# A new order for the opening of a fused attention and gated-MLP kernel, with eight PSUM banks instead of six up to the first output tile

## The chip, the cores, the metric

One core of a Trainium2 chip. The metric is the device time of one execution in microseconds (us); less is better. Times inside a trace are counted from the first instruction of the program, and the span of a trace is about 1.8 us shorter than the time of the run that it profiles.

Names used below: PE is TensorE, DVE is VectorE, ACT is ScalarE, POOL is GpSimd. A *bank* is one of the eight 128x512 float32 tiles of PSUM into which PE writes its results. A *slice* is one pass of four 128x512 matmuls that makes gate and value of 128 hidden features for one batch (`gv`). A *projection unit* (`c` or `u`) multiplies the small state with a block of columns of both weights (`c`) or of one (`u`). The *steady part* begins with slice 4 of batch 2 and runs to the end.

## The reference

```python
# x (8, 8, 512, 64), state (8, 8, 32, 64)
scores = scale * x @ state^T ;  a = softmax(scores) ;  xread = a @ state
scores2 = scale * state @ x^T ; a2 = softmax(scores2) ; sread = a2 @ x
y = concat([xread, sread], axis=2) -> rows of (B*S, H*D) = (4352, 512)
out = (relu(y @ w_gate) * (y @ w_val)) @ w_out        # d_ff = 1536, float32 result
```

The softmax works over 32 state entries, so `xread @ w` is computed as `a @ (state @ w)`: the projection units make `U = state @ w`, and a slice multiplies the transposed softmax with a block of `U`.

## The kernel before

The opening is written by hand as a list of words. Each word is a step; the digits after `@` are the PSUM banks that it takes, and a bank comes free when the step that evicts it has run.

```python
def bank(name, kind="r"):
    if given:
        n = given.pop(0)                       # the digits after "@"
    elif kind == "spare":
        n = 6 + turn["o"] % 2
    else:
        n = turn["r"] % 6 if kind == "r" else 6 + turn["o"] % 2   # steady part: a ring of six, two for outputs
        turn[kind] += 1
    return psum.tile([128, 512], FP32, name=name, tag=f"b{n}")

def x_load(b, part, parts):                    # dx: x in bf16, from the software queue of POOL
    ...
    nc.gpsimd.dma_start(out=xb[b][:, :, hs]..., in_=x[b, hs]...)

def x_T2(b, half):                             # xT2: PE transposes of x
    ...
    nc.tensor.transpose(ps[64 * h2:64 * h2 + 64, c, j], xb[b][:, c, 4 * half + 2 * j + h2], id128)

def state_conv(g, half, eng):                  # stc: state to bf16, on POOL for the later groups
    dst, src, keep = st_b[:, g % 3, :, half], st_f[:, g], odd[:, half:half + 1]
    ...
def state_T(g): ...                            # stT: PE transposes of a state group
def spin(n, cols=512):                         # warming matmuls with no use of their result
    for i in range(n):
        nc.tensor.matmul(warm_ps[:, 0:cols], warm[:, 0:128], warm[:, 0:cols], start=True, stop=True)

program = """
dx.1.0.2 dx.1.1.2 stc.0.0.act stc.0.1.dve spin.7 stT.0@0 xc.0.0.dve dw.0.0.128 sto.0.act ...
... c.1.512.256@54 mu.0.2 gv.1.2@21 ... c.0.512.256@30 re.1.2 gv.1.5@45 ...
... c.0.1024.256@41 c.0.1280.256@35 ... xT2.2.0@2 stc.1.0.pool ... xT2.2.1@0 stc.1.1.pool ...
... gv.0.5@41 ... gv.0.10@53 ... stT.1@2 ...
"""
```

Other words: `dw` loads a block of weight columns, `ds` the rest of the state, `do` the output weight; `sc` scores, `ex` exponential, `nr` sums and reciprocals, `nx` scaling; `aT`/`ao` transposes of the softmax; `co`/`uo` evictions of projection units; `re`/`mu` ReLU on ACT and product on DVE after a slice; `o` a third of an output tile; `sr`/`sn` the state read.

The softmax here doesn't subtract the row's maximum and nothing guards it: scores larger than these inputs give would overflow.

Of the kernel before, what the change touches and what calls it, by code (L numbers as in the profile page):

```python
# [16 lines left out]
def kernel(  # L17
# [52 lines left out]
    stT = const.tile([128, B, NJ, 64], BF16, name="stT")  # L70
# [5 lines left out]
    xf, xb, xT, e_sn, a_sn, ANS, U, hsb, sr_sb = {}, {}, {}, {}, {}, {}, {}, {}, {}  # L76
# [362 lines left out]
             "c": c_unit, "co": c_out, "u": u_unit, "uo": u_out, "gv": gv, "re": relu, "mu": mult, "o": out_part,  # L439
             "of": fin_x, "xn": x_next, "xp": x_pad, "sr": sr_mm, "sn": sr_norm}  # L440
    program = """
    dx.1.0.2 dx.1.1.2 stc.0.0.act stc.0.1.dve spin.7 stT.0@0 xc.0.0.dve dw.0.0.128 sto.0.act dw.1.0.128 on xc.0.1.dve
    spin.3 xT.0.1@1 dw.0.128.128 xT.0.0@2 xo.0.1.dve xo.0.0.act dw.1.128.128 spin.3 sc.0.0@3 dw.0.256.256 ex.0.0
    spin.1 xT.0.2@4 xT.0.3@5 xo.0.2.dve dw.1.256.256 xo.0.3.act nr.0.0 spin.3 sc.0.1@0 dw.0.512.256 xT2.1.0@1 ex.0.1
    nx.0.0 xo2.1.0.act nr.0.1 dw.1.512.256 spin.2 xT2.1.1@2 xo2.1.1.act sc.1.0@3 dw.0.768.256 nx.0.1 ex.1.0
    dw.1.768.256 spin.2 c.1.0.128@45 c.0.0.128@01 co.1.0.128.0.dve aT.0.1@2 co.0.0.128.0.act aT.0.0@3 co.1.0.128.1.dve
    co.0.0.128.1.act dw.0.1024.256 sc.1.1@4 ao.0.1.dve ao.0.0.act nr.1.0 ex.1.1 dw.1.1024.256 spin.2 c.0.128.128@05
    gv.0.0@12 co.0.128.128.1.act nr.1.1 co.0.128.128.0.act nx.1.0.pool re.0.0 gv.0.1@34 mu.0.0 re.0.1 nx.1.1.pool
    c.1.128.128@50 mu.0.1 co.1.128.128.1.act c.0.256.256@12 co.1.128.128.0.act c.1.256.256@30 dw.0.1280.256
    co.0.256.256.0.dve co.0.256.256.1.act aT.1.1@5 aT.1.0@4 co.1.256.256.0.act co.1.256.256.1.dve dw.1.1280.256  # L450
    gv.0.3@21 ao.1.1.act ao.1.0.dve dx.2.0.1 re.0.3 gv.0.2@30 mu.0.3 ds re.0.2 c.1.512.256@54 mu.0.2 gv.1.2@21
    co.1.512.256.1.act co.1.512.256.0.act do.0.6 c.0.512.256@30 re.1.2 gv.1.5@45 co.0.512.256.0.dve xp.1
    co.0.512.256.1.act mu.1.2 re.1.5 gv.1.3@23 mu.1.5 re.1.3 gv.1.1@04 do.6.12 mu.1.3 re.1.1 c.1.768.256@15 xp.0
    mu.1.1 gv.1.4@23 co.1.768.256.0.act co.1.768.256.1.act c.0.768.256@04 re.1.4 gv.1.0@15 co.0.768.256.0.dve
    co.0.768.256.1.act df.3 mu.1.4 re.1.0 gv.1.6@20 mu.1.0 re.1.6 gv.0.4@41 mu.1.6 re.0.4 gv.0.6@35 mu.0.4 re.0.6
    gv.1.7@20 mu.0.6 re.1.7 c.0.1024.256@41 c.0.1280.256@35 mu.1.7 co.0.1024.256.0.act xT2.2.0@2 stc.1.0.pool
    co.0.1024.256.1.act co.0.1280.256.1.dve xT2.2.1@0 stc.1.1.pool co.0.1280.256.0.act xo2.2.0.dve gv.0.5@41
    stc.3.0.pool stc.3.1.pool xo2.2.1.dve re.0.5 stc.2.1.pool gv.0.10@53 stc.2.0.pool mu.0.5 re.0.10 stT.1@2 gv.0.9@40
    mu.0.10 sto.1.act re.0.9 sc.2.1@1 gv.0.8@52 ex.2.1 mu.0.9 re.0.8 nr.2.1 gv.0.11@34 re.0.11 mu.0.8 gv.0.7@10
    nx.2.1.pool mu.0.11 re.0.7 sc.2.0@5 o.0.0@6 mu.0.7 ex.2.0 nr.2.0 c.1.1280.256@32 c.1.1024.256@14  # L460
    co.1.1280.256.1.act u.2.1.1024@50 o.0.1 co.1.1024.256.0.dve co.1.1024.256.1.act nx.2.0.pool uo.2.1.1024.1.dve
    uo.2.1.1024.0.act o.0.2 co.1.1280.256.0.act u.2.0.0@21 xn.3 of.0.0.dve u.2.1.0@45 uo.2.0.0.1.act u.2.1.512@03
    uo.2.1.0.0.dve o.0.3@7 uo.2.1.0.1.act uo.2.0.0.0.dve uo.2.1.512.0.act aT.2.0@1 aT.2.1@4 uo.2.1.512.1.dve
    ao.2.0.act o.0.4 ao.2.1.act o.0.5 gv.2.1@50 of.0.1.act re.2.1 gv.1.10@23 mu.2.1 re.1.10 gv.1.11@14 mu.1.10 re.1.11
    gv.2.3@50 mu.1.11 re.2.3 gv.2.2@23 mu.2.3 re.2.2 u.2.0.1024@14 u.2.0.512@50 mu.2.2 uo.2.0.1024.1.act sr.0@2
    o.0.6@6 uo.2.0.512.1.act uo.2.0.512.0.dve sn.0 gv.1.9@34 uo.2.0.1024.0.dve re.1.9 gv.1.8@05 mu.1.9 re.1.8
    gv.2.0@21 mu.1.8 re.2.0 o.0.7 mu.2.0 o.0.8 o.0.9@7 of.0.2.dve sr.1@3 sn.1 xp.2 xp.3
    """
    for word in program.split():
        word, _, banks = word.partition("@")  # L470
# [107 lines left out]
```

## Time and profile before

| | before |
|---|---|
| time, first three runs | 226.04 us median (225.94 to 226.09) |
| span of the trace (of another run, of 225.65 us) | 223.9 us |
| PE busy | 96% of the span |
| first slice starts | 14.43 us |
| x of batch 2: issued, landed | 18.42, 30.91 us |
| transposes of that x start | 30.96 us |
| state transposes start | 33.90 us |
| steady part starts | 57.28 us |

The lines that carry this stand in the prediction. The table is read from below: from 57.28 us on PE has no holes in this trace, so anything the change does to the time it must do to this moment.

### The profile page before, as it was taken

How to read it: one execution, taken by the hardware profiler on the slowest of the kernel's cores; microseconds unless marked ns; L12 is line 12 of the kernel's file. 1: busy time of each engine (PE TensorE's matmuls, PEld its weight loads, DVE VectorE, ACT ScalarE, POOL GpSimd, SP SyncE). 2: the span in 40 equal slices, each digit the busy share in tenths (PEclk: the TensorE clock that was granted, in tenths of full speed). 3: DMA queues.
4: the chain of work that ended last, by engine and by line, in shares of the span. 5: the costliest groups of instructions: out<-in, count | busy, mean ns of one | idle time of the engine just before them, and what ended most of it. 6: DMA issues, size and time to landing. Idle time of an engine off the chain costs nothing.

```text
span 223.9 us, 4840 instructions
## 1 busy us (share of the span) xinstructions
PE 215.5 (96%) x1937; PEld 105.8 (47%) x1967; DVE 129.0 (58%) x226; ACT 124.8 (56%) x236; POOL 53.0 (24%) x58
## 2 busy tenths in 40 slices
PE   7899999999999999999999999999999999999994
PEld 2544354444544444444444444444444445666543
DVE  3587888757595648663876468646874433222100
ACT  4599877865467644665557456545655444222221
POOL 8698828503302434006000700000000000000000
PEclk9999999999999999999999999999999999999999
DMA  7999999070146671781159114511311111111132
GB/s 157 176 195 197 215 225 278 24 187 3 47 106 225 112 267 47 160 265 50 50 118 276 49 60 99 107 50 47 94 50 47 48 47 50 48 64 74 54 94 94
DMA packets 37799, 25.48 MB, mean 114 GB/s; under 512 B 18864, under 2 KB 33200, under 8 KB 37776
## 3 DMA queue, kind: packets, MB, share of 16 engines
q1 hardware_dynamic: 24912, 16.85, 26.2%
q0 software_dynamic: 11968, 7.47, 21.5%
q10 hardware_dynamic: 896, 0.85, 1.4%
q8 instruction: 15, 0.25, 0.4%
q14 instruction: 8, 0.07, 0.1%
HBM read 18.35 MB, written 8.91 MB: 122 GB/s over the span
## 4 chain that ended last, share of the span: by engine, by line
PE 84%; DMA 9%; POOL 4%; issue 2%; DVE 0%; POOLq 0%; DVEq 0%
PE o_ps L353 38%; PE gv_ps L316 31%; DMA xb<-in_x_dram 9%; PE gv_ps L333 5%; PE up L291 4%; PE sr_ps L264 1%; POOL wv_sb L110 1%; PE sc_ps L200 1%; PE o_ps L379 1%; POOL wg_sb L110 1%; POOL a_sn L219 1%; PE xT_ps L186 0%; POOL xb L412 0%; PE stT_ps L129 0%; POOL xb L420 0%
## 5 line engine op out<-in xcount | busy, mean ns | idle before, releaser
L316 PE MATMUL gv_ps<-ans,U 128*128 128x512 bf16 x373 | 93.9, 380 | 0.5
L353 PE MATMUL o_ps<-wo_sb,h_sb 128*128 128x512 bf16 x357 | 91.6, 380 | 2.1 <-issue 1.9
L344 DVE TENSOR_TENSOR h_sb<-gv_ps,g_sb 128x512 bf16<-128x512 f32 x96 | 65.3, 689 | 44.2 <-ACT g_sb L340 43.3
L340 ACT ACTIVATE g_sb<-gv_ps 128x512 bf16<-128x512 f32 (+1 forms) x108 | 62.7, 580 | 49.3 <-PE gv_ps L316 34.5
L316 PEld LDWEIGHTS <-U 128*128 128x128 bf16 x384 | 35.8, 98 | 40.5 <-issue 0.6
L353 PEld LDWEIGHTS <-h_sb 128*128 128x128 bf16 x372 | 35.2, 98 | 39.9 <-issue 1.7
L361 ACT COPY o_sb<-o_ps 128x512 f32<-128x512 f32 x29 | 17.1, 590 | 16.5 <-PE o_ps L353 16.5
L301 ACT CAST U<-up 128x512 bf16<-128x512 f32 x36 | 18.9, 594 | 11.4 <-PE up L291 11.4
L301 DVE CAST U<-up 128x512 bf16<-128x512 f32 x36 | 22.8, 684 | 2.2 <-PE up L291 1.9
L142 POOL CAST xb<-xf 128x1024 bf16<-128x1024 f32 x10 | 10.1, 1040 | 53.6 <-DMA xf<-in_x_dram 32.6
L256 POOL COPY xa<-xb 128x2048 bf16<-128x2048 bf16 (+1 forms) x9 | 15.7, 1747 | 11.5 <-issue 6.6
L213 DVE TENSOR_REDUCE cs<-e_sn 128x16 f32<-128x512 bf16 x16 | 10.9, 683 | 7.7 <-ACT e_sn L207 7.7
L344 DVE TENSOR_TENSOR hs_sb<-gv_ps,g_sb 128x256 bf16<-128x256 f32 x12 | 5.1, 425 | 15.3 <-PE gv_ps L333 10.5
L207 ACT ACTIVATE e_sn<-sc_ps 128x512 bf16<-128x512 f32 x16 | 9.6, 600 | 5.6 <-PE sc_ps L200 5.5
L291 PEld LDWEIGHTS <-stT 64*32 64x32 bf16 x512 | 5.7, 90 | 11.2 <-issue 10.0
L311 ACT CAST U<-upc 128x512 bf16<-128x512 f32 (+1 forms) x20 | 9.6, 532 | 1.4 <-PE upc L291 1.3
L219 DVE TENSOR_TENSOR a_sn<-e_sn,rc 128x512 bf16<-128x512 bf16 x12 | 8.5, 709 | 0.6
L432 PE MATMUL warm_ps<-hs_sb 128*128 128x512 bf16 x20 | 7.2, 470 | 1.4 <-DVE hs_sb L396 1.2
L200 PEld LDWEIGHTS <-xT 128*128 128x128 bf16 x128 | 5.7, 98 | 3.8 <-ACT xT L177 0.7
L291 PE MATMUL up<-wg_sb,stT 64*32 64x512 bf16 x144 | 7.4, 383 | 0.0
L333 PE MATMUL gv_ps<-br,wg_sb 128*128 128x256 bf16 x48 | 7.2, 273 | 0.1
L333 PE MATMUL gv_ps<-br,wv_sb 128*128 128x256 bf16 x48 | 7.2, 273 | 0.0
(64 smaller groups left out, 129.5 us busy)
## 6 DMA issues: line engine op xcount, KB each, us to landing
out_dram<-o_sb SPq DMA_DIRECT2D x31, 256.0 KB, 2.3
xf<-in_x_dram SPq DMA_DIRECT2D x4, 1024.0 KB, 6.0
wo_sb<-in_moe_w_out_dram POOLq DMA_DIRECT2D x2, 768.0 KB, 15.4
wg_sb<-in_moe_w_gate_dram POOLq DMA_DIRECT2D x5, 256.0 KB, 8.7
wv_sb<-in_moe_w_val_dram POOLq DMA_DIRECT2D x5, 256.0 KB, 10.5
xf<-in_x_dram POOLq DMA_DIRECT2D x1, 1024.0 KB, 16.0
xb<-in_x_dram POOLq DMA_DIRECT2D x3, 256.0 KB, 7.1
xb<-in_x_dram POOLq DMA_DIRECT2D x1, 512.0 KB, 12.5
```

The lines of the kernel that those rows point to most:

```text
L142: copy[eng](out=xb[b][:, :, hs].rearrange("p c h d -> p h c d"), in_=xf[b][:, hs])
L213: nc.vector.reduce_sum(out=cs, in_=e_v, axis=AX.X)
L219: {"dve": nc.vector, "pool": nc.gpsimd}[eng].tensor_tensor(out=by_pair(a_sn[b], jp).rearrange("p r (j n) -> p r j n", n=Ns), in0=e_v, in1= ...
L256: nc.gpsimd.tensor_copy(out=v[:, hs:hs + src.shape[1]], in_=src)
L291: nc.tensor.matmul(dst[parity][32 * j:32 * j + 32], stT[r:r + 64, b, j, 32 * parity:32 * parity + 32], wsb[r:r + 64, j, lo:lo + n], start= ...
L301: copy[eng](out=U[b][:, w, kc, lo:lo + 512], in_=held["u", b, w, lo][kc])
L316: nc.tensor.matmul(ps[w], U[b][:, w, kc, f0:f0 + 128], ANS[b][:, kc].rearrange("p c t -> p (c t)"), start=(kc == 0), stop=(kc == NK - 1))
L333: nc.tensor.matmul(ps[w][:, 0:nt], wsb[:, j, f0:f0 + 128], br[:, j].rearrange("p b n -> p (b n)"), start=(j == 0), stop=(j == NJ - 1))
L340: nc.scalar.activation(out=g_sb[:, 0:n], in_=ps[0][:, 0:n], func=AF.Relu)
L344: nc.vector.tensor_tensor(out=dst, in0=ps[1][:, 0:n], in1=held["g", b, jf][:, 0:n], op=ALU.mult)
L353: nc.tensor.matmul(held["o", b, tsub], src[:, jf, tsub * 128:(tsub + 1) * 128], wo_sb[:, jf], start=(jf == 0), stop=(jf == NF - 1))
L361: copy[eng](out=o_sb, in_=held["o", b, tsub])
```

## The change

The intent: give the opening all eight banks until the first output tile needs two of them, let a search reorder it, and rename the ring banks at its end so that the steady slices begin on those that come free first. The diff replaces the whole list of words; its core, with cuts marked:

```diff
-    dx.1.0.2 dx.1.1.2 stc.0.0.act stc.0.1.dve spin.7 stT.0@0 xc.0.0.dve dw.0.0.128 sto.0.act dw.1.0.128 on xc.0.1.dve
-    spin.3 xT.0.1@1 dw.0.128.128 xT.0.0@2 xo.0.1.dve xo.0.0.act dw.1.128.128 spin.3 sc.0.0@3 dw.0.256.256 ex.0.0
-    ...
-    re.0.1 nx.1.1.pool  ...  c.1.512.256@54 mu.0.2 gv.1.2@21 ... c.0.512.256@30 re.1.2 gv.1.5@45
-    ... c.0.1024.256@41 c.0.1280.256@35 ... xT2.2.0@2 ... xT2.2.1@0 ... gv.0.5@41 ... gv.0.10@53 ... stT.1@2
-    ... gv.2.0@21 mu.1.8 re.2.0 o.0.7 mu.2.0 o.0.8 o.0.9@7 of.0.2.dve sr.1@3 sn.1 xp.2 xp.3
+    dx.1.0.2 dx.1.1.2 stc.0.0.act stc.0.1.dve xc.0.0.act dw.0.0.128 spin.6 stT.0@5 xT.0.0@0 xc.0.1.dve dw.1.0.128 on
+    sto.0.dve xT.0.1@4 xo.0.0.dve dw.0.128.128 xo.0.1.act dw.1.128.128 dw.0.256.256 spin.4 xT.0.3@2 dw.1.256.256
+    ...
+    re.0.0 ... nx.1.1 re.0.1 nx.1.0  ...  c.1.512.256@45 c.0.512.256@27 ... gv.1.1@03 ... gv.1.4@14 ... gv.1.3@57
+    ... c.1.1280.256@01 c.0.1280.256@57 ... xT2.2.1@3 ... xT2.2.0@2 ... c.1.768.256@46 ... c.1.1024.256@17
+    ... gv.1.10@05 ... stT.1@3 gv.1.11@42 ...
+    ... o.0.9@7 mu.2.3 sr.0@4 sr.1@5 sn.0 sn.1 xp.2 xp.3
```

The amount of useful work is the same. There are 15 warming matmuls instead of 23; the scalings of batches 1 and 2 (`nx`) run on DVE instead of POOL.

More of the change, by code (lines that the diff above doesn't have):

```diff
@@ L441 @@
     program = """
-    dx.1.0.2 dx.1.1.2 stc.0.0.act stc.0.1.dve spin.7 stT.0@0 xc.0.0.dve dw.0.0.128 sto.0.act dw.1.0.128 on xc.0.1.dve
-    spin.3 xT.0.1@1 dw.0.128.128 xT.0.0@2 xo.0.1.dve xo.0.0.act dw.1.128.128 spin.3 sc.0.0@3 dw.0.256.256 ex.0.0
-    spin.1 xT.0.2@4 xT.0.3@5 xo.0.2.dve dw.1.256.256 xo.0.3.act nr.0.0 spin.3 sc.0.1@0 dw.0.512.256 xT2.1.0@1 ex.0.1
-    nx.0.0 xo2.1.0.act nr.0.1 dw.1.512.256 spin.2 xT2.1.1@2 xo2.1.1.act sc.1.0@3 dw.0.768.256 nx.0.1 ex.1.0
-    dw.1.768.256 spin.2 c.1.0.128@45 c.0.0.128@01 co.1.0.128.0.dve aT.0.1@2 co.0.0.128.0.act aT.0.0@3 co.1.0.128.1.dve
@@ L447 @@
-    co.0.0.128.1.act dw.0.1024.256 sc.1.1@4 ao.0.1.dve ao.0.0.act nr.1.0 ex.1.1 dw.1.1024.256 spin.2 c.0.128.128@05
-    gv.0.0@12 co.0.128.128.1.act nr.1.1 co.0.128.128.0.act nx.1.0.pool re.0.0 gv.0.1@34 mu.0.0 re.0.1 nx.1.1.pool
-    c.1.128.128@50 mu.0.1 co.1.128.128.1.act c.0.256.256@12 co.1.128.128.0.act c.1.256.256@30 dw.0.1280.256
-    co.0.256.256.0.dve co.0.256.256.1.act aT.1.1@5 aT.1.0@4 co.1.256.256.0.act co.1.256.256.1.dve dw.1.1280.256
-    gv.0.3@21 ao.1.1.act ao.1.0.dve dx.2.0.1 re.0.3 gv.0.2@30 mu.0.3 ds re.0.2 c.1.512.256@54 mu.0.2 gv.1.2@21
@@ L452 @@
-    co.1.512.256.1.act co.1.512.256.0.act do.0.6 c.0.512.256@30 re.1.2 gv.1.5@45 co.0.512.256.0.dve xp.1
-    co.0.512.256.1.act mu.1.2 re.1.5 gv.1.3@23 mu.1.5 re.1.3 gv.1.1@04 do.6.12 mu.1.3 re.1.1 c.1.768.256@15 xp.0
-    mu.1.1 gv.1.4@23 co.1.768.256.0.act co.1.768.256.1.act c.0.768.256@04 re.1.4 gv.1.0@15 co.0.768.256.0.dve
-    co.0.768.256.1.act df.3 mu.1.4 re.1.0 gv.1.6@20 mu.1.0 re.1.6 gv.0.4@41 mu.1.6 re.0.4 gv.0.6@35 mu.0.4 re.0.6
-    gv.1.7@20 mu.0.6 re.1.7 c.0.1024.256@41 c.0.1280.256@35 mu.1.7 co.0.1024.256.0.act xT2.2.0@2 stc.1.0.pool
@@ L457 @@
-    co.0.1024.256.1.act co.0.1280.256.1.dve xT2.2.1@0 stc.1.1.pool co.0.1280.256.0.act xo2.2.0.dve gv.0.5@41
-    stc.3.0.pool stc.3.1.pool xo2.2.1.dve re.0.5 stc.2.1.pool gv.0.10@53 stc.2.0.pool mu.0.5 re.0.10 stT.1@2 gv.0.9@40
-    mu.0.10 sto.1.act re.0.9 sc.2.1@1 gv.0.8@52 ex.2.1 mu.0.9 re.0.8 nr.2.1 gv.0.11@34 re.0.11 mu.0.8 gv.0.7@10
-    nx.2.1.pool mu.0.11 re.0.7 sc.2.0@5 o.0.0@6 mu.0.7 ex.2.0 nr.2.0 c.1.1280.256@32 c.1.1024.256@14
-    co.1.1280.256.1.act u.2.1.1024@50 o.0.1 co.1.1024.256.0.dve co.1.1024.256.1.act nx.2.0.pool uo.2.1.1024.1.dve
@@ L462 @@
-    uo.2.1.1024.0.act o.0.2 co.1.1280.256.0.act u.2.0.0@21 xn.3 of.0.0.dve u.2.1.0@45 uo.2.0.0.1.act u.2.1.512@03
-    uo.2.1.0.0.dve o.0.3@7 uo.2.1.0.1.act uo.2.0.0.0.dve uo.2.1.512.0.act aT.2.0@1 aT.2.1@4 uo.2.1.512.1.dve
-    ao.2.0.act o.0.4 ao.2.1.act o.0.5 gv.2.1@50 of.0.1.act re.2.1 gv.1.10@23 mu.2.1 re.1.10 gv.1.11@14 mu.1.10 re.1.11
-    gv.2.3@50 mu.1.11 re.2.3 gv.2.2@23 mu.2.3 re.2.2 u.2.0.1024@14 u.2.0.512@50 mu.2.2 uo.2.0.1024.1.act sr.0@2
-    o.0.6@6 uo.2.0.512.1.act uo.2.0.512.0.dve sn.0 gv.1.9@34 uo.2.0.1024.0.dve re.1.9 gv.1.8@05 mu.1.9 re.1.8
@@ L467 @@
-    gv.2.0@21 mu.1.8 re.2.0 o.0.7 mu.2.0 o.0.8 o.0.9@7 of.0.2.dve sr.1@3 sn.1 xp.2 xp.3
+    dx.1.0.2 dx.1.1.2 stc.0.0.act stc.0.1.dve xc.0.0.act dw.0.0.128 spin.6 stT.0@5 xT.0.0@0 xc.0.1.dve dw.1.0.128 on
+    sto.0.dve xT.0.1@4 xo.0.0.dve dw.0.128.128 xo.0.1.act dw.1.128.128 dw.0.256.256 spin.4 xT.0.3@2 dw.1.256.256
+    xT.0.2@3 xo.0.3.dve sc.0.0@1 xo.0.2.act ex.0.0 sc.0.1@6 dw.0.512.256 xT2.1.0@5 ex.0.1 nr.0.0 xo2.1.0.act
+    dw.1.512.256 spin.2 xT2.1.1@0 nr.0.1 xo2.1.1.act sc.1.0@4 dw.0.768.256 nx.0.0 dw.1.768.256 ex.1.0 spin.2
@@ new lines @@
+    c.1.0.128@23 nx.0.1 sc.1.1@1 co.1.0.128.1.act c.0.0.128@65 co.1.0.128.0.dve dw.0.1024.256 aT.0.1@0 ex.1.1
+    co.0.0.128.0.dve aT.0.0@4 co.0.0.128.1.act ao.0.1.dve dw.1.1024.256 ao.0.0.act spin.1 c.1.128.128@32 nr.1.1
+    c.0.128.128@16 co.1.128.128.1.act gv.0.0@50 co.0.128.128.0.act nr.1.0 co.0.128.128.1.act dw.0.1280.256 re.0.0
+    gv.0.1@42 co.1.128.128.0.act nx.1.1 re.0.1 nx.1.0 dw.1.1280.256 c.0.256.256@17 c.1.256.256@65 co.0.256.256.1.act
+    co.0.256.256.0.dve aT.1.0@3 aT.1.1@4 co.1.256.256.0.act ao.1.0.dve gv.0.2@71 dx.2.0.1 ao.1.1.dve
@@ new lines @@
+    co.1.256.256.1.act mu.0.1 re.0.2 gv.1.0@36 mu.0.0 ds re.1.0 mu.0.2 c.1.512.256@45 c.0.512.256@27
+    co.1.512.256.0.act co.1.512.256.1.dve gv.1.1@03 co.0.512.256.1.act do.0.6 co.0.512.256.0.dve re.1.1 gv.1.4@14
+    mu.1.0 xp.0 re.1.4 gv.1.3@57 mu.1.1 re.1.3 mu.1.4 gv.0.5@20 mu.1.3 do.6.12 re.0.5 gv.0.3@61 mu.0.5 xp.1 re.0.3
+    c.0.768.256@35 c.0.1024.256@47 mu.0.3 co.0.768.256.1.act gv.1.2@20 co.0.1024.256.1.act co.0.768.256.0.dve df.3
+    re.1.2 gv.0.4@61 co.0.1024.256.0.dve re.0.4 mu.1.2 gv.1.5@57 mu.0.4 re.1.5 gv.0.9@32 mu.1.5 re.0.9 gv.0.8@46
@@ new lines @@
+    mu.0.9 re.0.8 c.1.1280.256@01 c.0.1280.256@57 mu.0.8 co.1.1280.256.1.act xT2.2.1@3 co.0.1280.256.1.act
+    co.1.1280.256.0.dve xT2.2.0@2 stc.1.0.pool co.0.1280.256.0.act c.1.768.256@46 xo2.2.1.dve stc.1.1.pool
+    c.1.1024.256@17 xo2.2.0.act stc.3.0.pool gv.1.10@05 co.1.768.256.0.dve stc.2.0.pool co.1.768.256.1.dve
+    co.1.1024.256.1.act stc.2.1.pool stT.1@3 gv.1.11@42 stc.3.1.pool re.1.10 sto.1.dve co.1.1024.256.0.act mu.1.10
+    gv.0.11@76 re.1.11 re.0.11 mu.1.11 gv.1.7@30 mu.0.11 re.1.7 gv.1.9@15 mu.1.7 re.1.9 sc.2.0@4 gv.0.7@72 mu.1.9
@@ new lines @@
+    ex.2.0 re.0.7 nr.2.0 gv.0.6@36 re.0.6 mu.0.7 gv.0.10@01 mu.0.6 re.0.10 u.2.0.0@45 u.2.1.512@73 nx.2.0
+    uo.2.0.0.1.act u.2.0.512@20 o.0.0@6 mu.0.10 uo.2.0.512.1.act uo.2.1.512.0.act uo.2.0.0.0.dve sc.2.1@5 o.0.1
+    uo.2.0.512.0.act xn.3 uo.2.1.512.1.dve ex.2.1 u.2.1.1024@01 nr.2.1 u.2.1.0@42 uo.2.1.1024.0.act u.2.0.1024@35
+    o.0.2 uo.2.1.0.1.act uo.2.0.1024.1.dve uo.2.1.0.0.act o.0.3@7 nx.2.1 of.0.0.dve aT.2.1@0 gv.1.8@25
+    uo.2.1.1024.1.dve ao.2.1.act re.1.8 uo.2.0.1024.0.dve aT.2.0@4 o.0.4 ao.2.0.dve mu.1.8 gv.2.0@01 re.2.0 o.0.5
@@ L468 @@
+    mu.2.0 gv.2.2@23 of.0.1.act re.2.2 gv.1.6@45 mu.2.2 re.1.6 o.0.6@6 mu.1.6 o.0.7 o.0.8 gv.2.1@01 of.0.2.dve re.2.1
+    gv.2.3@23 mu.2.1 re.2.3 o.0.9@7 mu.2.3 sr.0@4 sr.1@5 sn.0 sn.1 xp.2 xp.3
     """
```

## The prediction

> **What bounds the kernel now.** I read the page first, then the chain that ended last, then the timelines of TensorE (PE) and of GpSimd (POOL) around the places that the chain names, and last the order of the instructions on each engine in the changed program. From the page:
>
> ```profile
> PE 215.5 (96%) x1937; PEld 105.8 (47%) x1967; DVE 129.0 (58%) x226; ACT 124.8 (56%) x236; POOL 53.0 (24%) x58
> ...
> PE   7899999999999999999999999999999999999994
> ...
> DMA  7999999070146671781159114511311111111132
> ```
>
> PE is the engine of the span, and its row dips only in the first two slices (11 us). The DMA row is full over the first seven slices (up to 39 us) and thin afterwards. So there are two regimes: a beginning in which weights and inputs arrive as PE uses them, and a long steady part. In the steady part a pair of four 512-column matmuls (gate and value of one slice, then a piece of the output) takes 1.73 us, and the starts in the trace leave no hole between 58 us and the tail. The change touches only the hand-written program before that part, so what matters is when the first steady slice starts: 57.28 us before.
>
> The chain for the beginning:
>
> ```profile
> 14.09 0.69 POOL wv_sb L110
> ...
> 14.89 0.89 POOL a_sn L219
> 15.90 1.04 POOL a_sn L219
> 16.94 0.75 POOL wg_sb L110
> 17.69 0.73 POOL wv_sb L110
> 18.42 12.49 DMA xb<-in_x_dram
> 30.91 0.04 issue
> 30.96 1.08 PE xT_ps L186 x32
> ```
>
> It runs through the load of batch 2's x: issued at 18.42, landed at 30.91, and PE transposes it at once at 30.96. Then the PE timeline around it, and POOL's:
>
> ```profile
> 30.57 0.29 PE L291 MATMUL upc<-wv_sb,stT 64*32 64x256 bf16 x8
> 30.96 1.08 PE L186 MATMUL xT_ps<-id,xb 128*64 128x128 bf16 x32
> 31.97 1.90 PE L316 MATMUL gv_ps<-ans,U 128*128 128x512 bf16 x7
> 33.90 0.40 PE L129 MATMUL stT_ps<-id,st_b 128*128 128x128 bf16 x4
> ```
>
> ```profile
> 32.01 5.43 POOL L124 TENSOR_SCALAR st_b<-st_f,odd 128x256 bf16<-128x256 f32 x6 [4.81 <-DMA st_f<-in_state_dram]
> ```
>
> PE had finished its earlier work at 30.86, so it reaches the transposes within 0.1 us of the data. At 33.90 comes a second meeting: the transposes of the second state group need two POOL conversions of 0.91 us (5.43 / 6) after the state's landing at 31.92, so they cannot start before 33.84. These two times, 30.91 and 33.84, are set by loads and not by banks.
>
> **What the Trainium skill says.** "TensorE: Matmul & The Clock Gate", section "Back-to-back issue gap", gives N / 2.4 + 2.5 ns for an isolated matmul, 216 ns at N = 512, and a lower sustained figure of about 131 ns. The trace agrees with the first (four matmuls start every 0.863 us) and not with the second; 0.863 us is my unit below. The same page, "What's actually happening", says that PE starts at half clock and is released after about 3.4 us of activity: here the first seven warming matmuls start 0.43 us apart and from 5.0 us they start 0.22 us apart. That is what the warming matmuls are for. "Perfetto Trace Analysis", section "Matmuls", asks for independent groups to rotate through PSUM banks so that eviction overlaps matmuls, which is the intent of using eight banks instead of six. Here six already do: the waits of PE from 14 to 58 us list only 0.3 us, put down to issue. "DMA: Bandwidth & Descriptors", section "Two DMAs through the same engine are not ordered", says that the descriptors of a queue start in order; so a load behind a full backlog does not land sooner for being issued sooner. The trace fits: the queue moves about 190 GB/s from 5 to 25 us without a pause, and the 256 KB weight loads land about 1.35 us apart.
>
> **The change part by part.** The work on PE is the same: 28 slices of gate and value, 10 output pieces, 14 + 6 projection units, the same transposes. Only the order, the banks and the engines of some evictions differ, and 15 warming matmuls stand where 23 stood.
>
> 1. *Eight warming matmuls less.* At 0.22 to 0.43 us they are 1.7 to 3.4 us of PE, but they fill waits before the first slice (14.43 us). They are worth nothing by themselves.
>
> 2. *The head up to the first slice.* The new order puts batch 0's first score block behind the late x transposes (data at 8.20), so that both blocks' softmax work follows together on VectorE (DVE). By durations of the old trace: last copy of x ends near 9.5, exponentials end near 10.1 and 10.7, two sums with reciprocals (0.68 + 0.25 each) end near 12.0, two scalings (0.70 each) near 13.4; before, the second scaling ended at 12.34. Transposes, two copies and evictions put the first slice near 14.9, half a microsecond later.
>
> 3. *Batch 1's scalings move from POOL (0.89 + 1.04 us) to DVE (2 x 0.70 us).* POOL issues batch 2's x by the landing it must wait for, 17.85, instead of 18.42. With the backlog above I give that nothing. On DVE the 1.4 us lie just where the first evictions are, so batch 1's weight transposes wait until about 17.9 (17.44 before) and a later slice waits about 0.4 us for an eviction.
>
> 4. *What absorbs this.* The new program asks for the 1024 column block as its second projection after nine slices; that weight lands at 25.56. My walk brings PE there at about 25.7. Then five slices (4.3 us), two projections (0.5 us) and a few transitions (0.1 us each) bring it to x of batch 2 at 30.7 to 31.2. When it gets there both programs have done the same 14 slices and 12 projection units. So this meeting moves by -0.05 to +0.3 us.
>
> 5. *From there to the steady part.* The old one goes transposes, 2 slices, state transposes at 33.90. The new one goes transposes (1.02), two projections (0.46), transition (0.1), 1 slice (0.86): 30.95 + 2.44 = 33.4, and waits 0.5 us for POOL. From the state transposes on, the old one took 57.28 - 33.90 = 23.38 us. The new one has left: state transposes 0.23; 13 slices and 10 output pieces, 23 x 0.863 = 19.85; two score blocks 0.46; six u units 1.36; score transposes 0.45; two state reads 0.74; sum 23.09. To this come about four changes between narrow and full-width matmuls at 0.1 us, since u units stand in threes, and 0.1 us for a DVE scaling just ahead of its transposes: 23.6 us. I checked the banks by name on this stretch: each is free 0.1 us or more before its matmul. So the steady part starts at 33.90 + 23.6 = 57.5, 0.2 us later than before. Because the state conversion fixes 33.84, a delay of up to 0.5 us in step 4 does not add to this.
>
> 6. *Steady part.* The renamed ring begins on banks freed first. Since the old trace shows no hole after 58 us, there is nothing for this to win: 0.
>
> Sum: 226.04 + 0.2 = 226.2 us.
>
> **The rivals.** (a) *Loads land earlier.* If POOL's two scalings did hold up the queue, x and the state come up to 0.57 us earlier and the whole steady part with them: about 225.5. For it: the chain walks through these two instructions. Against it: a full queue and 12.49 us from issue to landing. (b) *DVE becomes the bound.* With 1.4 us more DVE work where it was already 4.28 of 5 us busy (15 to 20 us), evictions could hold PE by a microsecond before x of batch 2; less the 0.5 us of cover, 226.7 to 227.2. (c) *Eight banks free PE from waits that the trace hides*, such as the transitions between 31 and 57 us. The old stretch from 30.96 lasts 26.32 us for 25.4 us of work, so at most 0.9 us is there to win: 225.1 at the very best. (d) *Half clock.* With fewer warming matmuls PE may leave the head at 0.43 us per matmul, or fall back; every slice in a slow stretch costs 0.86 us more, so one to two microseconds, partly covered: up to 227.5. I give it one in ten, because the six first ones still fill 1.2 to 3.8 us.
>
> **Range and chances.** The signs are mixed and every term is below 1 us, against 4.5 us for 2%. Centre 226.2; (a) and (c) make the low end 225.3, (b) and (d) the high end 227.1. Within 2%: 0.97; slower by more than 2% needs (b) and (d) together and more, 0.02; faster 0.01, as no more than 0.9 us is idle after the meeting with the load.
>
> **What would show it.** Right: x of batch 2 lands within 0.3 us of 30.9; its transposes start with it; the state transposes start near 33.9 after a wait of about 0.5 us; the first steady slice starts at 57.2 to 57.9; from there to the end 166.6 us, as now. Step 2 is wrong if the first slice starts before 14.4, step 3 if x lands below 30.5. The prediction is wrong as a whole if the steady part starts outside 56.5 to 58.4, or if it has holes of its own, which only the new bank order could bring.

## The result

The changed kernel took 224.75 us (224.55 to 224.80, 4 runs) beside 225.99 us (225.82 to 226.09) for the kernel before: ratio 0.9944, interval 0.9927 to 0.9961. Ratios here are the mean time of one kernel's fast runs over that of the other's of the same rounds, so they are not quite the ratio of the medians quoted. By the 2% rule this is as forecast; but the time lies outside my range of 225.3 to 227.1, and the sign of the step is the opposite.

First the page of the changed kernel, the rows that the prediction quoted of before (PE and its 40 slices, and the DMA slices):

```profile
PE 217.4 (98%) x1959; PEld 106.9 (48%) x1959; DVE 131.1 (59%) x233; ACT 123.2 (55%) x233; POOL 48.9 (22%) x54
...
PE   6999999999999999999999999999999999999994
...
DMA  6999999152046771771169114511311111111132
```

The picture is the same. Next the PE timeline of the changed kernel around the transposes of batch 2's x, with POOL's line of the state conversions (columns: start us, us from first start to last end, engine, line, operation, count):

```profile
30.29 0.29 PE L291 MATMUL upc<-wv_sb,stT 64*32 64x256 bf16 x8
30.51 1.08 PE L186 MATMUL xT_ps<-id,xb 128*64 128x128 bf16 x32
...
32.09 1.04 PE L316 MATMUL gv_ps<-ans,U 128*128 128x512 bf16 x4
32.96 0.39 PE L129 MATMUL stT_ps<-id,st_b 128*128 128x128 bf16 x4
```

```profile
30.30 5.45 POOL L124 TENSOR_SCALAR st_b<-st_f,odd 128x256 bf16<-128x256 f32 x6 [4.13 <-DMA st_f<-in_state_dram]
```

Three things differ from my forecast. POOL starts converting at 30.30 where it started at 32.01, because the state landed 1.7 us earlier. So nothing waits before the state transposes, where I had expected 0.5 us. And PE reaches the transposes of x at 30.51, when their data had been there since 29.19. The steady part starts at 56.45 instead of 57.28. That is 0.83 us of the 0.93 us that the spans differ by (the other 0.1 us is in the steady part: 166.50 us against 166.60). The medians differ by 1.24 us; the rest of that is in no trace, as the trace of before is of a faster run (225.65 us) than the four quoted.

My rival (a) had foreseen earlier loads, through POOL's freed scalings. But the very first load of that queue, long before those scalings, already landed at 6.83 instead of 8.20 us, although POOL handled it at the same time in both kernels. POOL's timeline, the kernel before and then the changed one:

```profile
1.42 0.98 POOL L412 DMA_DIRECT2D xb<-in_x_dram  x1
```

```profile
1.43 0.95 POOL L412 DMA_DIRECT2D xb<-in_x_dram  x1
```

So either something early in the program had moved the loads, or the landing differs from execution to execution. This had to be asked first.

A third observation: in this trace PE was still at half clock when it came to the second group of warming matmuls. The PE timeline of the changed kernel's start:

```profile
1.18 2.74 PE L432 MATMUL warm_ps<-hs_sb 128*128 128x512 bf16 x6 [1.18 <-DVE hs_sb L396]
4.54 0.61 PE L129 MATMUL stT_ps<-id,st_b 128*128 128x128 bf16 x4 [0.63 <-ACT st_b L121]
...
6.12 1.91 PE L432 MATMUL warm_ps<-hs_sb 128*128 128x512 bf16 x4
```

Four matmuls in 1.91 us start 0.43 us apart (6.12, 6.54, 6.97, 7.39). My rival (d) came true here: the first slice starts at 15.12 us, the latest of all traces, and still the kernel was faster. It was not free, though: PE comes to the value weights of columns 256 to 511 at 17.05, 1.64 us after they landed (15.41), where in every other trace it starts on them within about 0.2 us of their landing; what this cost is worked out near the end.

### The profile page after: what moved, and what is told of

The parts are those of the page before. It is cut to its first block, busy times and chain, and to the rows that moved or that the text cites. A ratio compares the mean times of both kernels' runs of the same rounds, so it can differ in the third digit from the quotient of the medians.

```text
span 222.9 us, 4842 instructions
## 1 busy us (share of the span) xinstructions
PE 217.4 (98%) x1959; PEld 106.9 (48%) x1959; DVE 131.1 (59%) x233; ACT 123.2 (55%) x233; POOL 48.9 (22%) x54
## 4 chain that ended last, share of the span: by engine, by line
PE 95%; ACT 2%; DMA 1%; issue 0%; DVE 0%; DVEq 0%; ACTq 0%
PE o_ps L353 39%; PE gv_ps L316 38%; PE gv_ps L333 5%; PE up L291 4%; PE sc_ps L200 2%; DMA st_f<-in_state_dram 1%; PE sr_ps L264 1%; PE upc L291 1%; PE o_ps L379 1%; PE warm_ps L432 1%; PE xT_ps L186 1%; PE stT_ps L129 1%; PE xT_ps L169 1%; PE xT_ps L173 0%; ACT xT L189 0%; ACT e_sn L207 0%
## 5 line engine op out<-in xcount | busy, mean ns | idle before, releaser
L353 PE MATMUL o_ps<-wo_sb,h_sb 128*128 128x512 bf16 x372 | 94.8, 379 | 0.0
L301 DVE CAST U<-up 128x512 bf16<-128x512 f32 x35 | 22.0, 682 | 2.3 <-PE up L291 1.9
L219 DVE TENSOR_TENSOR a_sn<-e_sn,rc 128x512 bf16<-128x512 bf16 x16 | 11.4, 723 | 0.3
L311 ACT CAST U<-upc 128x512 bf16<-128x512 f32 (+1 forms) x18 | 8.7, 542 | 0.9 <-PE upc L291 0.9
L432 PE MATMUL warm_ps<-hs_sb 128*128 128x512 bf16 x15 | 6.2, 548 | 1.2 <-DVE hs_sb L396 1.2
```

Source lines behind the costliest of these rows:

```text
L219: {"dve": nc.vector, "pool": nc.gpsimd}[eng].tensor_tensor(out=by_pair(a_sn[b], jp).rearrange("p r (j n) -> p r j n", n=Ns), in0=e_v, in1= ...
L301: copy[eng](out=U[b][:, w, kc, lo:lo + 512], in_=held["u", b, w, lo][kc])
L353: nc.tensor.matmul(held["o", b, tsub], src[:, jf, tsub * 128:(tsub + 1) * 128], wo_sb[:, jf], start=(jf == 0), stop=(jf == NF - 1))
```

## The experiments

I give for each trace the moments that my argument needs; the table stands at the end of this section.

### The two kernels again, unchanged

> The kernel before, unchanged. It tells whether the landing of the loads is a property of the program or of the execution. Theory 1 (the late landing belongs to the program): batch 0's late half of x lands at 8.2 us and batch 2's x at 30.9, within 0.2, as in the first trace; steady part starts at 57.3; 226.0 us. Rival (chance of the execution): x lands anywhere between 29.2 and 30.9 while the time stays within 0.3 us, because TensorE gets there only at 30.86.

> The changed kernel, unchanged. Theory 1 (program): batch 0's late half of x lands at 6.8 us, batch 2's x at 29.2, the state at 30.2, steady part from 56.45; 224.75 us. Rival (chance): the loads land at other times, up to 30.9 for x and 31.9 for the state, and then the state transposes wait up to 0.9 us and the time of that execution is up to 225.6.

On this second chip the kernel before took 225.16 us (224.93 to 225.60, 7 runs), its copy 224.88 (224.56 to 225.16, 4 runs; ratio 0.9985, interval 0.9968 to 1.0003), and the changed kernel 224.48 (224.18 to 225.04; 0.9971, 0.9950 to 0.9992). The landing of x in the copy of the kernel before was 29.36, not 30.91; in the changed kernel 30.27, not 29.19. So the landing is no property of the program: it differs by 1.55 us in this pair of traces, and my theory 1 of this experiment fell. This pair ran on two chips; but two later runs on one chip, a_after2 and g_state_later, whose programs differ only in what follows this load, have x land at 29.15 and 30.70. So it scatters between executions.

What an early landing does to the old order is seen in the PE timeline of the unchanged kernel before on this chip:

```profile
29.99 0.29 PE L291 MATMUL upc<-wv_sb,stT 64*32 64x256 bf16 x8
30.21 1.13 PE L186 MATMUL xT_ps<-id,xb 128*64 128x128 bf16 x32
31.27 1.90 PE L316 MATMUL gv_ps<-ans,U 128*128 128x512 bf16 x7
33.01 0.39 PE L129 MATMUL stT_ps<-id,st_b 128*128 128x128 bf16 x4
```

x had landed at 29.36 and POOL's second conversion ended at 32.32, so neither is waited for: the old order is now bound by its own stream of matmuls. In the trace that I predicted from, data and PE had met within 0.1 us by coincidence.

### The early evictions swapped; batch 1's scalings back on POOL

```diff
 # b_head_copies, on the kernel before
-    spin.7 stT.0@0 xc.0.0.dve dw.0.0.128 sto.0.act dw.1.0.128 on xc.0.1.dve
+    spin.7 stT.0@0 xc.0.0.act dw.0.0.128 dw.1.0.128 on xc.0.1.dve sto.0.dve
 # c_pool_scalings, on the changed kernel
-    nx.1.1 re.0.1 nx.1.0 dw.1.1280.256
+    nx.1.1.pool re.0.1 nx.1.0.pool dw.1.1280.256
```

> The kernel before with only the two early evictions swapped as in the change: the first cast of x goes to ScalarE and the copy of the state transposes to VectorE. If VectorE's casts from 4.2 to 5.6 us held back the first software queue loads, the late half of x lands near 6.8 instead of 8.2 and batch 2's x near 29.3, and the time falls by 0.1 to 0.3 us, as TensorE is ready at 30.86. If they have nothing to do with it: 8.2, 30.9, and 226.0.

> The changed kernel with batch 1's two scalings back on GpSimd. If these two held up the queue (my rival a), x of batch 2 lands 0.5 us or more later than in the changed kernel and the state transposes start later; time up to 225.3. If the backlog hides them, the landings stay (29.2 and 30.2) and the time is 224.6 to 224.8, perhaps less, as VectorE is relieved of 1.4 us.

Swapped evictions: x landed at 29.42, as early as in the unchanged copy, and the time was 225.11 us (0.9994, 0.9977 to 1.0012). No effect on the time; the landing alone would have looked like a success if the copy had not been run beside it.

Scalings on POOL: x landed at 29.55, inside the scatter of the changed kernel (29.15 to 30.27 over its four traces), 224.74 us (0.9979, 0.9962 to 0.9995). POOL issued the load at 17.81 where it was 17.36 (a_after2) and 17.53 (first trace) with the scalings on DVE. One trace could not show a shift of half a microsecond in such a scatter, but all of them together can be compared: leaving out the two with an extra load (below), x landed at 29.77 in the mean of seven traces with these scalings on POOL and at 29.69 in the mean of nine with them on DVE. So nothing is left of rival (a) that shows, in landing or in time; a shift of a few tenths is not excluded. The scalings on POOL cost PE a small wait before batch 1's transposes, as the list of its waits says (columns: us in total, times, longest):

```profile
PE aT_ps L235 <- POOL a_sn L219: 0.3, 1, 0.3
```

### The waits for the two late loads taken away

```diff
 # n_before and n_after: wrong result on purpose (relative error 1.25), loads unchanged
-    nc.tensor.transpose(ps[...], xb[b][:, c, 4 * half + 2 * j + h2], id128)
+    nc.tensor.transpose(ps[...], xb[1][:, c, 4 * half + 2 * j + h2], id128)
-    dst, src, keep = st_b[:, g % 3, :, half], st_f[:, g], odd[:, half:half + 1]
+    dst, src, keep = st_b[:, g % 3, :, half], st_f[:, 0], odd[:, half:half + 1]
```

> Wrong result on purpose: the kernel before, its late transposes of batch 2's x reading batch 1's x, and the later state conversions reading the first state group, so that no TensorE work waits for the two late loads; the loads themselves stay. Theory 1 (the orders differ little; the landing decides): the steady part starts at 56.1 to 56.5 whatever the loads do, time 0.1 to 0.3 us below the kernel before. Rival (the new order is better by itself): see n_after.

> Wrong result on purpose: the changed kernel with the same two waits removed. If the new order and its eight banks win by themselves, this is 0.3 to 0.6 us below n_before (fewer switches between narrow and wide matmuls, fewer waits for weights), with the transposes of x started at 29.9 to 30.3 and the steady part at 55.8 to 56.1. If the change gained only from loads that landed early by chance, it is within 0.15 us of n_before.

225.06 us (224.50 to 225.70) and 224.21 us (223.98 to 224.32), both beside 225.19 for the kernel before on the third chip: 0.9997 (0.9966 to 1.0028) and 0.9957 (0.9940 to 0.9974). With nothing to wait for at these two places the new order is 0.8 us faster by the medians, more than the 0.3 to 0.6 expected, but two of the four runs of n_before are a full microsecond slower than the other two, so the size is uncertain. In the two profiled executions the steady part starts at 56.15 and 55.85, only 0.3 us apart; but in n_after the value weights that both wait for had landed 0.42 us later (16.41 against 15.99). Counted from that landing it is 40.16 and 39.44 us, 0.72 us apart. The gain is in the order. That n_before still scatters by 1.2 us (224.50 to 225.70) also says that the waits for these two loads are not the only source of scatter; its slow runs were not profiled.

Where it is, the traces tell if each is measured from the moment at which the value weights of columns 256 to 511 land, which all but the first trace of the changed kernel run into near 16 us. From this landing to the transposes of x the old order needs 13.96 to 14.04 us and the new one 13.51 us, whenever nothing is waited for in between (13.66 with the warming matmuls put back, where PE comes 0.1 us late, and 13.70 with batch 1's scalings on POOL, with the wait just shown). Both do the same matmuls there. What differs is how often PE changes between the narrow projection matmuls and the full-width slices. PE timeline of the kernel before (first profile), one such visit:

```profile
19.92 0.29 PE L291 MATMUL upc<-wv_sb,stT 64*32 64x256 bf16 x8
20.15 1.04 PE L316 MATMUL gv_ps<-ans,U 128*128 128x512 bf16 x4
21.11 0.30 PE L291 MATMUL upc<-wg_sb,stT 64*32 64x256 bf16 x8
```

And of the changed kernel on the third chip, from the wait for the value weights to the transposes of x, where two units stand together and five slices follow:

```profile
16.02 0.30 PE L291 MATMUL upc<-wv_sb,stT 64*32 64x256 bf16 x8 [0.20 <-DMA wv_sb<-in_moe_w_val_dram]
...
19.30 0.29 PE L291 MATMUL upc<-wv_sb,stT 64*32 64x256 bf16 x8
19.52 4.49 PE L316 MATMUL gv_ps<-ans,U 128*128 128x512 bf16 x20
23.95 0.30 PE L291 MATMUL upc<-wg_sb,stT 64*32 64x256 bf16 x8
...
29.49 1.08 PE L186 MATMUL xT_ps<-id,xb 128*64 128x128 bf16 x32
```

A group of eight narrow matmuls inside a run takes 0.11 us to the next start; the last before a slice takes 0.22 to 0.23. Twenty slice matmuls take 4.43 us to the next start where 20 x 0.2158 = 4.32 us would do, and a single slice takes 0.96 instead of 0.863. So each visit costs about 0.1 us going in and 0.1 us coming out. The old order makes five such visits between these two points and the new one three: 2 x 0.22 = 0.44 us, of the 0.46 us measured. This is an account by measured durations; no run changed the number of visits and nothing else. The Trainium skill names a likely reason on the page "TensorEngine Tiling (Array Packing)", section "Key Properties": changing the tiling mode drains TensorE. It gives no figure; here a change costs 0.1 us each way. A further 0.24 us lies between the transposes of x and the steady part (26.17 us in n_before, 25.93 in n_after), where the new order again makes fewer visits; I have not taken it apart.

### Both loads made late

```diff
 # l_before and l_after
+    def dummy_load():                      # 256 KB into a tile that is rewritten at about 40 us
+        u_alloc(2)
+        nc.gpsimd.dma_start(out=U[2][:, 0, 0, 0:1024]..., in_=moe_w_gate...[:, :, 0:256])
-    ... dx.2.0.1 ...
+    ... dd dx.2.0.1 ...
```

> The kernel before with one more 256 KB load (into a tile that is rewritten later) ahead of batch 2's x, so that x and the state land 1.35 us later whatever the execution: x at 30.7 to 31.6. Theory 1: the steady part starts at 57.1 or later, time 0.3 to 0.8 us over the kernel before.

> The changed kernel with the same extra load. My recorded walk: with the late landing its state transposes wait about 0.5 us and its steady part starts 0 to 0.3 us later than that of l_before, so the time is 0 to 0.3 us over l_before. Rival (the new order wins also when loads are late): 0.3 us or more under l_before.

225.76 us (225.42 to 226.91; 1.0042, 1.0007 to 1.0078) and 225.72 us (225.28 to 226.35; 1.0028, 1.0003 to 1.0052). The two orders cannot be told apart when the loads are late: what I had predicted. PE timelines, l_before and then l_after:

```profile
30.80 1.08 PE L186 MATMUL xT_ps<-id,xb 128*64 128x128 bf16 x32
31.82 1.90 PE L316 MATMUL gv_ps<-ans,U 128*128 128x512 bf16 x8
33.77 0.40 PE L129 MATMUL stT_ps<-id,st_b 128*128 128x128 bf16 x4
```

```profile
31.20 1.08 PE L186 MATMUL xT_ps<-id,xb 128*64 128x128 bf16 x32 [1.08 <-DMA xb<-in_x_dram]
...
32.78 1.04 PE L316 MATMUL gv_ps<-ans,U 128*128 128x512 bf16 x4
34.16 0.40 PE L129 MATMUL stT_ps<-id,st_b 128*128 128x128 bf16 x4 [0.35 <-POOL st_b L124]
```

Both come to the state transposes 2.96 to 2.97 us after those of x, set by POOL. The new order arrives early and spends its advantage in two waits: 1.08 us for x and 0.35 us for POOL.

### Banks alone, the renaming, and the state transposes one slice later

```diff
 # e_eight_banks: kernel before, order untouched, 42 words get other bank digits (eight in turn)
-    c.0.128.128@05 gv.0.0@12 ... gv.0.1@34 ...
+    c.0.128.128@35 gv.0.0@46 ... gv.0.1@01 ...
 # f_late_ring: changed kernel, banks 0,1 and 4,5 exchanged in every word
-    gv.2.3@23 mu.2.1 re.2.3 o.0.9@7 mu.2.3 sr.0@4 sr.1@5 sn.0 sn.1
+    gv.2.3@23 mu.2.1 re.2.3 o.0.9@7 mu.2.3 sr.0@0 sr.1@1 sn.0 sn.1
 # g_state_later: changed kernel
-    stT.1@3 gv.1.11@42
+    gv.1.11@42 stT.1@3
```

> The changed kernel unchanged, once more, for the scatter of the landings and a better ratio. Theory 1 (the order is 0.4 us better when loads are early, equal when late): 0.3 to 0.7 us under the kernel before of this chip; the state transposes start at 32.4 to 33.9, and the first steady slice 23.5 us after them in every execution.

> The kernel before, same order on every engine, with only the bank numbers up to four tiles before the first output changed: eight banks in turn, least recently freed first, instead of six. If banks were what the change won by, this gains 0.3 us or more on the kernel before. Theory 1: no wait of TensorE in the old trace is for a bank, so within 0.15 us of the kernel before, and the distance from the transposes of x to those of the state stays 2.80 us.

> The changed kernel with ring banks 0,1 and 4,5 exchanged throughout, so that the first steady slice takes the two banks of the state reads, which are freed last. If the renaming matters, this slice waits for VectorE: 0.4 to 0.5 us later in the trace (distance from the state transposes to the steady part 23.9 to 24.0 instead of 23.5) and in time. If it does not matter, no difference.

> The changed kernel with the state transposes one slice later, so that GpSimd's two conversions have 0.86 us more. Theory 1 (what sets the start of the steady part is the state conversion when loads are late): transposes never wait for GpSimd, time 0 to 0.5 us under the changed kernel, most where loads land late, and its runs scatter less. If the state conversion does not bound, no difference.

The changed kernel again: 224.32 us (223.94 to 225.59, 6 runs) beside 225.18 (0.9976, 0.9948 to 1.0005).

Eight banks alone: 225.28 us (1.0008, 0.9982 to 1.0034). The distance between the two sets of transposes is 2.76 us instead of 2.80, and between the weight landing and the transposes of x 13.96, the same as with six. From the state transposes to the steady part it takes 23.61 instead of 23.38 us, perhaps because the bank digits that I left behind the first output fit worse; I did not look. Banks by themselves were not what the old order lacked.

The renaming undone in the worst way: the PE timeline shows the first steady slice waiting for the state read to leave its bank.

```profile
55.53 0.71 PE L264 MATMUL sr_ps<-xa,e_sn 128*32 128x65 bf16 x64
56.58 1.04 PE L316 MATMUL gv_ps<-ans,U 128*128 128x512 bf16 x4 [0.35 <-DVE sn L273]
```

The distance from the state transposes to the steady part is 23.91 us instead of 23.49, as expected. In time it is 224.82 us (0.9983, 0.9968 to 0.9997), which this many runs do not separate from the changed kernel's 0.9976. So the renaming guards against a wait of 0.4 us that a careless naming would bring in; the kernel before had no such wait, so the change wins nothing by it.

State transposes later: 224.09 us (0.9959, 0.9936 to 0.9983). In its trace x landed late, at 30.70, and yet the transposes of the state wait for nothing; the steady part started at 56.78, where l_before with x at 30.76 started at 57.15.

### Once more, with the warming matmuls put back

```diff
 # h_spins, on the changed kernel: 23 warming matmuls instead of 15
-    spin.6 ... spin.4 ... spin.2 ... spin.2 ... spin.1
+    spin.7 ... spin.7 ... spin.4 ... spin.4 ... spin.1
 # g_state_later2 is g_state_later again; a_before2 and a_after3 are the two kernels unchanged
```

> The kernel before, once more. From the rule of the traces so far (steady part starts at the state transposes plus 23.4 us; they start at the later of x transposes + 2.80 and the second conversion): if x lands before 30.1, state transposes at 32.8 to 33.1 and 224.6 to 224.9 us; if it lands at 30.9, 33.9 and 225.7. A share of its runs over 225.4 means late landings here too.

> The changed kernel, once more. If the landing has the same scatter for both programs, the state transposes start at 32.1 to 32.9 for x before 29.9 and up to 33.9 for x at 30.9; time 0.3 to 0.7 us under a_before2. If the program itself made the loads land earlier, x would land before 29.9 in every trace of it (it already landed at 30.27 in one).

> The changed kernel with 23 warming matmuls instead of 15 (one more at the start, three more before the late x, two more in two later places). My recorded step 1: they fill waits and are worth nothing, so the time is within 0.15 us of a_after3, and the first slice starts within 0.7 us of it, absorbed by the wait for the weights that land at 16.2. Rival: the eight removed ones are where the gain is, then this is 0.4 us or more over a_after3.

> The state transposes one slice later, again beside the changed kernel on the same chip: 0.1 to 0.4 us under a_after3 if the wait for GpSimd's conversions is the last one left, no difference if not.

On the fourth chip: kernel before 225.08 us (224.43 to 225.93, 11 runs), its copy 225.01 (0.9995, 0.9965 to 1.0025), the changed kernel 224.47 (223.87 to 225.49; 0.9972, 0.9939 to 1.0004), with the warming matmuls back 224.59 (0.9971, 0.9942 to 1.0001; one run of 227.52 was slow and is left out), state transposes later 224.19 (0.9956, 0.9926 to 0.9986). The warming matmuls are no part of the gain: the first slice starts 0.7 us later with them (14.40), the transposes of x at 29.88 against 30.01. The question about the landing is answered too: x landed at 30.01 in the kernel before and at 29.84 in the changed one, with a spread inside each program larger than any difference between them.

a_before2 was profiled in a run of 225.30 us, although its state transposes started at 33.01 like those of a_before, whose run took 224.75. The difference is a stall at 88 us. PE timelines, a_before2 and then a_before:

```profile
88.75 0.39 PE L291 MATMUL up<-wg_sb,stT 64*32 64x512 bf16 x1
89.33 0.41 PE L291 MATMUL up<-wg_sb,stT 64*32 64x512 bf16 x7 [0.19 <-DVE h_sb L344]
89.67 1.04 PE L353 MATMUL o_ps<-wo_sb,h_sb 128*128 128x512 bf16 x4
```

```profile
88.71 0.45 PE L291 MATMUL up<-wg_sb,stT 64*32 64x512 bf16 x8
89.33 0.81 PE L353 MATMUL o_ps<-wo_sb,h_sb 128*128 128x512 bf16 x3 [0.16 <-issue]
```

(In the last line the first record of four is missing, so the output piece began at 89.1.) This stall of 0.57 us appears in three of the eighteen traces, with the old order (a_before2, b_head_copies) and with the new (h_spins): a second source of scatter, not of this change. What ends it I have not found; the profile puts part of it to DVE and the rest to nothing that it shows.

### The moments of the traces in one table

| trace | value weights 256-511 landed | x of batch 2 landed | second state conversion ends | transposes of x | state transposes | steady part |
|---|---|---|---|---|---|---|
| before (first) | 16.82 | 30.91 | 33.84 | 30.96 | 33.90 | 57.28 |
| a_before | 16.24 | 29.36 | 32.32 | 30.21 | 33.01 | 56.38 |
| a_before2 | 16.16 | 30.01 | 32.96 | 30.13 | 33.01 | 56.40 |
| n_before | 15.99 | 29.13 | not waited for | 29.98 | 32.77 | 56.15 |
| l_before | 16.25 | 30.76 | 33.71 | 30.80 | 33.77 | 57.15 |
| after (first) | 15.41 | 29.19 | 32.14 | 30.51 | 32.96 | 56.45 |
| a_after | 16.25 | 30.27 | 33.21 | 30.32 | 33.27 | 56.76 |
| a_after2 | 15.98 | 29.15 | 32.10 | 29.49 | 32.16 | 55.65 |
| a_after3 | 16.50 | 29.84 | 32.80 | 30.01 | 32.86 | 56.35 |
| n_after | 16.41 | 29.64 | not waited for | 29.92 | 32.37 | 55.85 |
| l_after | 16.45 | 31.16 | 34.10 | 31.20 | 34.16 | 57.65 |
| g_state_later | 17.34 | 30.70 | 33.65 | 30.85 | 34.16 | 56.78 |
| g_state_later2 | 16.23 | 29.38 | 32.32 | 29.74 | 33.06 | 55.68 |

The table obeys one rule (but for the state transposes of g_state_later and g_state_later2, which were moved on purpose). The transposes of x start at the later of two moments: x landed plus 0.05, or the weight landing plus 14.0 (old) or 13.5 (new; later only in the first trace of the changed kernel, with its late first slice). The state transposes start at the later of the transposes of x plus 2.80 (old) or 2.45 (new), and the end of the second conversion plus 0.06. The steady part follows 23.38 (old) or 23.49 (new) after the state transposes. With early loads the old order stands at 14.0 + 2.80 + 23.38 = 40.2 us after the weight landing. The new one could stand at 13.5 + 2.45 + 23.49 = 39.4, and in a_after2 and a_after3, where POOL's conversion binds, it is at 39.7 and 39.9. The landing of those weights scatters too (15.98 to 17.34 in the traces that run into it), and where PE binds, this passes on to the steady part in full. With late loads both stand at the conversion, and the old order is 0.1 us ahead.

Over the three later chips the changed kernel took 224.54 us in the mean of 16 runs and the kernel before 225.13 in the mean of 36 (standard errors 0.14 and 0.07): 0.6 us. The first measurement, 1.24 us, compared four runs of before that are all at the slow end of this scatter (225.8 to 226.1, where 36 later ones span 224.4 to 225.9) with four of after near its middle.

State transposes later took 224.20 in the mean of 12 runs (standard error 0.11) and is the best version tried. It beats the kernel before clearly. Over the changed kernel it is 0.3 us, about twice the error of that difference, so not settled by the times; the traces show what it can win: its steady part started 25.93 and 25.94 us after the transposes of x, in both loads' states, while the changed kernel needs up to 26.45 where POOL binds.

## Why the prediction was wrong

The step that failed is in its first part: "These two times, 30.91 and 33.84, are set by loads and not by banks." They were, in that execution. I then carried them through every later step as constants of the program, and step 5 closed the door with "Because the state conversion fixes 33.84". The same program has x land anywhere from 29.4 to 30.9 us, and in five of the six traces of the old order without the extra load PE itself, and not x, sets the start of the transposes. Only then does a shorter PE stream pay. Step 4's "-0.05 to +0.3 us" was in fact -0.46 us, counted from the landing of the value weights (13.51 us against 13.97). Nor did rival (c) cover this: its "at most 0.9 us" and "225.1 at the very best" look only behind 30.96, while this 0.46 us lies before it. By my own signs the miss was plain: x landed at 29.19, below 30.5, and the steady part began at 56.45, just under 56.5. But the first of these signs accused step 3, which was right; the early landing was chance.

Point by point:

- *Warming matmuls worth nothing* (step 1): right, as far as h_spins resolves it (224.56 us in the mean of its five fast runs, and 224.56 in the six of a_after3). *Half clock* (rival d): it is in the first trace of the changed kernel, which also has the latest first slice. PE came to the transposes of x 15.10 us after the value weights instead of 13.51, at 30.51. Without that delay x (29.19) and POOL's conversion (32.14) would have bound, and the state transposes would have started at 32.20 instead of 32.96 by the rule above: an estimate of 0.76 us lost, which the early loads more than made up. How much of the delay is the half clock was not separated: the first state transposes also waited 0.63 us for a conversion on ACT.
- *The head half a microsecond later* (step 2): right in mechanism. I had 14.9 for a late x landing at 8.20, which is 6.7 us after it; measured 6.6 to 6.9 us after that landing in the three later traces of the changed kernel. But those landings were at 6.9 to 7.5.
- *Nothing for POOL's freed scalings* (step 3): right for the load, as far as c_pool_scalings and the means of the landings (29.77 and 29.69) can show. That a full backlog hides the time of issue was my inference; the page that I cited speaks only of the order within one queue of one DMA engine. The delay that I added for DVE was too large.
- *Meeting the load* (step 4): wrong, as said. I had also counted the changes between narrow and full-width matmuls as "a few transitions" in the new order without counting those that the old one makes more of. By the account above they are 0.44 us, the largest single item of the gain.
- *From there to the steady part* (step 5): the terms were right. The new order has 2.45 us between the two sets of transposes (I had 2.44) and 23.49 us after them (I had 23.6). The forecast of equality with late loads was borne out by l_before and l_after.
- *The ring* (step 6): right, nothing won; f_late_ring shows what it prevents.
- *The range*: I took the median of three runs that lie within 0.15 us as the time of the program and put 0.2 us on top, though the trace that I worked from was of a run of 225.65 us, 0.4 us faster: a sign of scatter that I passed over. Loads that meet PE within 0.1 us are a warning that a small shift of either changes what binds; I read it as a proof that the load binds.

What stays open: why the software queue's loads land up to 1.55 us apart in programs that are the same up to them, why the four first runs of the kernel before were all slow (225.8 to 226.1), and what ends the stall at 88 us. In the first trace twelve of the sixteen completions of the first load come between 5.90 and 6.19 us and the last at 8.20, so one part of the transfer lags, but why no run here shows. I cannot exclude that on the first chip something favoured the changed program.

## What to carry to other kernels

When a profile shows data arriving within a tenth of a microsecond of the engine that needs it, take a second profile of the same program before calling the load the bound: one of the two may be a coincidence, and a change that shortens the engine's stream pays in those executions where the data is early. Group narrow (row- and column-tiled) matmuls together; each visit to them from full-width ones cost about 0.2 us here. And run the unchanged kernel beside every experiment: without it, the swapped evictions here would have been taken for the cause of early loads.

## What the Trainium skill lacked or had wrong

- "TensorEngine Tiling (Array Packing)", "Key Properties": says that a mode switch drains TensorE, but not what it costs. Here about 0.11 us into and 0.11 us out of a group of 64x32-tiled matmuls between 128x128 ones.
- "TensorE: Matmul & The Clock Gate", "Back-to-back issue gap": gives about 131 ns as the sustained spacing at N = 512. None of the three traces searched for it (the first two and a_after2) goes below 0.215 us; twenty in a row took 4.43 us including the switch. The formula for the isolated gap, 216 ns, which the page's section "Wait — 56ns, not 53.3ns?" also gives for back-to-back matmuls, is what holds in the stream.
- I found on none of the pages that I read how far the landing of the same load varies between executions. Here the first software-queue load landed between 6.8 and 8.2 us over all traces, and batch 2's x between 29.4 and 30.9 us in three traces of one unchanged program.
